# Attention with other halves transposed on TensorE, five low parts on VectorE, x's parts issued later, the first dense tiles placed anew, and w_out's last tile decoded into another buffer

## Chip, cores, metric

The kernel runs on one core of one Trainium2 chip. The metric is the device time of one execution in microseconds; lower is better.

## What is computed

Causal attention over 2 batches, 12 heads, 448 positions and a head size of 64, then a mixer over positions and channels, then a gated layer:

```python
scores = np.where(mask, -1e9, scale * q @ k.T)           # causal, softmax over keys
x = softmax(scores) @ v                                  # to (2, 448, 768)
h = np.maximum(xt @ w_tok1, 0.0) @ w_tok2                # xt: positions last; 448 -> 256 -> 448
u = x + h.transpose(0, 2, 1)
x = u + np.maximum(u @ w_ch1, 0.0) @ w_ch2               # 768 -> 1536 -> 768
h = gelu(x @ w_in)                                       # 768 -> 1024
uu, v = h[..., :512], h[..., 512:]
v_n = (v - mu) / sqrt(var + 1e-6) * g_ln
gated = uu * (w_sg @ v_n + b_sg)                         # over positions
out = x + gated @ w_out                                  # 512 -> 768
```

## The kernel before

**Precision.** Every operand is split into a high and a low part, and each product is three matmuls (hi by hi, hi by lo, lo by hi): `mm3`, L204 to L211. The weights come from memory as eight-byte words into `wraw` and are decoded in three steps (`decode`, L119): ScalarE writes `wm`, VectorE shifts it (L133) and puts in the low bits (L134). Then ScalarE copies the high part and GpSimd subtracts for the low part (`sub`, L103).

**Attention** works on pairs of heads; pair (b,n) is heads 2n and 2n+1 of batch b, `hd` is which of the two, and each head has two halves (`HALVES`, L229), of 512 columns of scores together. For each half `probabilities` (L349) lets TensorE write the scores (`s_ps`, two buffers, L367), VectorE add the mask and take the row maximum (L372: `pe`, `mx`), ScalarE take the exponential (L381). Then the half is transposed on one of two ways. By DMA: ScalarE copies the high part of `hl` (L393), GpSimd writes the low one (L394), SP issues the transpose into `pT` (L395). Or by TensorE (`on_pe`, L383): four transposes into `t_ps` (L387), the high copy on ScalarE (L389), the low part on VectorE (L390). `ON_PE` (L67) says which pairs do this, always for half 1 of head 1. `values` (L408) multiplies `pT` with v into `x_ps` (L418 to L420). At the end of a pair (L446 to L458) VectorE normalises into `xf`, ScalarE copies `xh`, GpSimd makes `xl` and the remaining pieces of `xh`. After two pairs `token_mix` (L460) runs: `a_ps` (L465, then mm3), and then `u_ps` and its parts `uh`, `ul`.

**v.** `prepare_v` (L507) loads v, VectorE takes its absolute maximum (`am`, L336), TensorE spreads it (`vm`, L338), VectorE makes the scale `sv` and the low part `vl` (L344).

**Order.** A scheduler orders every engine's instructions by program order and by the priority that `tc.high_priority(offset=...)` gives; a negative offset lets work give way to what comes after it. `tc.issue_after` puts an instruction behind another. Every DMA, the transposes included, is issued by SP in its own order. The first products with w_ch1 (`r_ps`) fill TensorE during attention: `THIRDS` (L66) says after which head how many thirds of a tile are issued (`up_third`), `BEHIND` (L65) behind which head's transpose each tile's load stands, `LATER` (L64) is the offset of that load's work. `up` takes the rest of the eight tiles NF0 after attention.

**After attention** the r tiles of w_ch1 run, then y with w_ch2, the gelu with w_in, the spatial gate `g_ps` (L855 to L872), and `o_ps` with w_out (L884). w_out's tiles are decoded one at a time by `begin16` into `wm` (three buffers), with a maximum (`wams`, L176), and scaled by `end16` (L198 to L202). At the end of a batch's gate `top_of` (L178) reduces four maxima `gtam` to one, which TensorE spreads into `gt_ps` (L188); `gate16` (L840) then splits the gate into `gt_hi` and `gt_lo` (L196).

Of the kernel before, what the change touches and what calls it, by code (L numbers as in the profile page):

```python
# [15 lines left out]
ALU = mybir.AluOpType  # L16
# [12 lines left out]
def mixer_kernel(  # L29
# [34 lines left out]
    LATER = 0  # L64
    BEHIND = [11, 13, 17, 16, 14, 15, 13, 15]  # L65
    THIRDS = {15: 2, 17: 1, 18: 2, 19: 1, 20: 2, 21: 2, 22: 3, 23: 2}  # L66
    ON_PE = [(0, 1), (0, 2), (0, 3), (0, 4), (0, 5), (1, 0), (1, 1), (1, 2), (1, 4)]  # L67
# [88 lines left out]
    def load_w(src, pool=wpool, bufs=3, behind=None):  # L156
# [7 lines left out]
        else:  # L164
# [3 lines left out]
            w = WC // 3  # L168
            for i in range(3):
                cs = slice(i * w, (i + 1) * w)  # L170
                sub(lo1[:, cs], m[:, cs], hi1[:, cs])
# [102 lines left out]
    with ExitStack() as at:  # L274
# [74 lines left out]
        def probabilities(qp, k2, hd, half, on_pe):  # L349
# [44 lines left out]
            nc.gpsimd.tensor_sub(hl[:, 1], pe, hl[:, 0])  # L394
# [27 lines left out]
        def pair(b, n, e, qk, x, on_pe):  # L422
# [3 lines left out]
            for hd in range(2):  # L426
                if (b, n) != (0, 0):
                    vh, vl, sv = vss[b, n]
                    for half in range(2):
                        values(px, probabilities(*qk, hd, half, on_pe and (hd, half) == (1, 1)), hd, half, vh, vl)  # L430
                else:
                    pTs = []
                    for half in range(2):
                        pTs.append(probabilities(*qk, hd, half, False))
# [19 lines left out]
            for h in range(2):
                hs, ls = (slice(64 * i, 64 * i + 64) for i in (h, 1 - h))
                ds = slice(e * P + h * D, e * P + h * D + D)
                nc.gpsimd.tensor_scalar(xh[hs, 0, ds], xf[hs, e, 0], 1.0, 0.0, ALU.mult, ALU.add)
                sub(xh[ls, 0, ds], xf[hs, e, 0], xh[hs, 0, ds])  # L458
# [62 lines left out]
        def up_third():  # L521
# [8 lines left out]
            with tc.high_priority(offset=-400):  # L530
# [17 lines left out]

        last_mx, last_s, v_begun, tok_raw = [None], [None], {}, {}
# [8 lines left out]
        for n, (b, h) in enumerate(order):  # L558
# [7 lines left out]
            if n == 2:  # L566
                with tc.high_priority(offset=-50):
# [265 lines left out]
    begin16(w_out[NDC + 1], NDC + NDC + 1)  # L833
# [110 lines left out]
```

## Time and profile before

| what | value |
|---|---|
| median of 3 runs | 412.0 us (411.12 to 412.44) |
| profiled execution | 410.7 us |
| its span, first to last instruction | 408.9 us |
| mean granted clock of TensorE | 0.996 |
| TensorE busy | 389.2 us (95%) |
| VectorE busy | 292.2 us (71%) |
| ScalarE busy | 250.7 us (61%) |
| GpSimd busy | 196.9 us (48%) |

The profiled execution is 1.3 us below the median of the runs, and its span leaves out 1.8 us around the instructions. TensorE is the busiest engine by far. A share of 95% is a mean over the program, though: the stretches show where the rest lies, and the list of waits what it waits for. In the rows, PE is TensorE, DVE VectorE, ACT ScalarE, POOL GpSimd, SP the engine that issues the DMAs.

### The profile page before, as it was taken

To read this page: it belongs to the slowest core of one execution; us is meant where nothing else is said; L and a number is where in the kernel's file an instruction comes from. 1 tells how busy PE (TensorE), PEld (TensorE's weight loads), DVE (VectorE), ACT (ScalarE), POOL (GpSimd) and SP (SyncE) were. 2 spreads that over 40 slices of the span, in tenths; PEclk is the share of its full clock that TensorE was granted. 3 is DMA by queue.
4 is the path that set the end of the run, shared out by engine and by line. 5 is a ranking of instruction groups with operands and counts; after the bars stand their busy time and mean duration, and the time that the engine had idled before them with its cause. 6 is when DMAs were issued, how large, how long until landed. Compare 5 with 4: busy or idle time off the path is not lost.

```text
span 408.9 us, 7351 instructions
## 1 busy us (share of the span) xinstructions
PE 389.2 (95%) x2638; PEld 267.5 (65%) x2638; DVE 292.2 (71%) x702; ACT 250.7 (61%) x479; POOL 196.9 (48%) x218
## 2 busy tenths in 40 slices
PE   5898899889998999999999999999999999998996
PEld 3565778678887989999887555555544445554454
DVE  5988986876885625534468787787799997569842
ACT  3887887686977546636689894534177265654200
POOL 3766775696889564341351355254112168315300
PEclk9998999999999999999999999999999999999999
DMA  7999989979967944556733403644621331100123
GB/s 237 207 231 239 229 168 230 231 145 262 226 184 171 232 158 127 183 179 212 243 102 115 145 11 96 206 136 128 230 61 31 103 104 52 53 1 0 69 97 106
DMA packets 57525, 60.74 MB, mean 149 GB/s; under 512 B 43665, under 2 KB 49041, under 8 KB 57489
## 3 DMA queue, kind: packets, MB, share of 16 engines
q1 hardware_dynamic: 57488, 60.28, 55.8%
q8 instruction: 21, 0.34, 0.3%
q14 instruction: 16, 0.12, 0.1%
HBM read 47.29 MB, written 2.75 MB: 122 GB/s over the span
## 4 chain that ended last, share of the span: by engine, by line
DVE 24%; ACT 15%; PE 14%; DMA 11%; issue 5%; POOL 4%; ACTq 0%; SPq 0%; POOLq 0%; DVEq 0%
DMA wraw<-in 11%; ACT r L195 3%; DVE wm L134 3%; PE o_ps L209 2%; ACT w L200 2%; PE o_ps L210 2%; DVE w2m L134 2%; PE o_ps L208 2%; DVE y L196 2%; DVE w2m L133 2%; ACT wm L130 2%; PE r_ps L208 2%; PE r_ps L209 2%; PE r_ps L210 1%; ACT w2m L130 1%
## 5 line engine op out<-in xcount | busy, mean ns | idle before, releaser
L367 PE MATMUL s_ps<-k,q 128*128 128x64 f32 (+3 forms) x216 | 54.9, 399 | 7.2 <-DMA q<-in 4.7
L104 POOL TENSOR_TENSOR wlo<-wm,whi 128x256 fp32r<-128x256 f32 (+1 forms) x36 | 42.4, 1198 | 37.1 <-ACT whi L143 32.1
L394 POOL TENSOR_TENSOR hl<-pe,hl 128x512 f16<-128x512 f32 x39 | 48.4, 1251 | 13.6 <-ACT hl L393 13.0
L208 PE MATMUL r_ps<-uh,whi 128*128 128x448 f32 x144 | 54.1, 377 | 0.0
L209 PE MATMUL r_ps<-ul,whi 128*128 128x448 f32 x144 | 53.3, 370 | 0.0
L210 PE MATMUL r_ps<-uh,wlo 128*128 128x448 f32 x144 | 52.9, 367 | 0.0
L208 PE MATMUL y_ps<-r,w 128*128 128x448 f16 x144 | 50.6, 353 | 0.0
L209 PE MATMUL y_ps<-r,w 128*128 128x448 f16 x144 | 50.6, 352 | 0.0
L210 PE MATMUL y_ps<-r,w 128*128 128x448 f16 x144 | 50.4, 352 | 0.0
L133 DVE TENSOR_SCALAR wm<-wm 128x768 int32<-128x768 int32 (+2 forms) x35 | 21.4, 612 | 38.4 <-ACT wm L130 38.4
L130 ACT ACTIVATE wm<-wraw 128x768 f32<-128x768 f32 (+2 forms) x35 | 27.8, 797 | 34.2 <-DMA wraw<-in 27.8
L367 PEld LDWEIGHTS s_ps<-k,q 128*128 128x128 f32 x216 | 31.4, 203 | 14.3 <-DVE vh L306 4.6
L372 DVE CUSTOM_DVE_ANT_0 pe<-s_ps,mask 128x192 f32<-128x192 f32 (+3 forms) x84 | 34.4, 442 | 5.6 <-PE s_ps L367 5.3
L134 DVE SCALAR_TENSOR_TENSOR wm<-wraw,wm 128x768 int32<-128x768 int32 (+2 forms) x35 | 37.6, 1074 | 0.6
L269 POOL TENSOR_TENSOR y<-yt,ul 128x448 f32<-128x448 f32 x10 | 13.2, 1323 | 42.3 <-DVE yt L267 42.3
L381 ACT ACTIVATE pe<-pe,bias 128x448 f32<-128x448 f32 (+3 forms) x66 | 31.5, 528 | 0.3
L418 PE MATMUL x_ps<-vh,pT 128*128 128x65 f16 (+1 forms) x240 | 25.9, 197 | 4.5 <-DMA pT<-hl 3.4
L209 PEld LDWEIGHTS r_ps<-ul,whi 128*128 128x128 f32 x144 | 27.1, 188 | 3.0 <-issue 0.6
L208 PEld LDWEIGHTS r_ps<-uh,whi 128*128 128x128 f32 x144 | 27.0, 188 | 2.8 <-issue 0.4
L210 PEld LDWEIGHTS r_ps<-uh,wlo 128*128 128x128 f32 x144 | 27.0, 188 | 2.7 <-issue 0.2
L202 POOL TENSOR_TENSOR w<-w2m,w 128x768 f16<-128x768 f32 x12 | 20.6, 1731 | 16.1 <-ACT w2m L201 13.2
L418 PEld LDWEIGHTS <-pT 128*128 128x128 f16 (+1 forms) x240 | 21.5, 99 | 10.3 <-DMA pT<-hl 4.8
(214 smaller groups left out, 1033.5 us busy)
## 6 DMA issues: line engine op xcount, KB each, us to landing
wraw<-in SPq DMA_DIRECT2D x36, 768.0 KB, 4.5
wraw<-in SPq DMA_DIRECT2D x14, 512.0 KB, 3.7
vr<-in SPq DMA_DIRECT2D x12, 320.0 KB, 4.3
k<-in SPq DMA_DIRECT2D x12, 224.0 KB, 3.7
q<-in SPq DMA_DIRECT2D x24, 112.0 KB, 3.9
out<-ob SPq DMA_DIRECT2D x11, 224.0 KB, 2.0
wraw<-in SPq DMA_DIRECT2D x3, 256.0 KB, 3.4
sgr<-in SPq DMA_DIRECT2D x3, 224.0 KB, 2.8
```

Source lines behind the costliest of these rows:

```text
L104: nc.gpsimd.tensor_sub(lo, src, f32(hi))
L130: nc.scalar.activation(m, words.bitcast(F32)[:, :, 1], AF.Prelu, scale=2.0 ** -112, alpha=-(2.0 ** 32))
L133: nc.vector.tensor_scalar(mi, mi, 3, None, ALU.logical_shift_left)
L134: nc.vector.scalar_tensor_tensor(mi, words[:, :, 0], 29, mi, ALU.logical_shift_right, ALU.bitwise_or)
L208: nc.tensor.matmul(ps, lh, rh, start=i == 0 and not begun, stop=False)
L209: nc.tensor.matmul(ps, lh, rl, start=False, stop=False)
L210: done.append(nc.tensor.matmul(ps, ll, rh, start=False, stop=ended and i == n - 1).ins)
L367: last_s[0] = nc.tensor.matmul(ps[:, o:o + m], qp[:, q0:q0 + P], k2[:, ks], start=True, stop=True).ins
L372: last_mx[0] = nc.vector.tensor_tensor_reduce(out=pe[:, cs], in0=ps[:, cs], in1=mask0 if i == 0 else mask[:, MASKS[i]], scale=-1.0 / math. ...
L381: nc.scalar.activation(pe[:, cs], pe[:, cs], AF.Exp, bias=bias[:, j:j + 1], scale=-1.0)
L394: nc.gpsimd.tensor_sub(hl[:, 1], pe, hl[:, 0])
L418: nc.tensor.matmul(o, ph, vh[:, c, h, :D + 1], start=j == 0, stop=False)
```

## The change

Which halves are transposed on TensorE is now a list of halves: (0,1), (1,1), (1,2) and (0,5) keep half 1 of head 1, (0,5) has half 1 of head 0 besides, and in (0,2), (0,3), (0,4), (1,0) it is another half than before; (1,4) has none any more. It is 9 halves as before. Five of the halves that go by DMA have their low part made by VectorE (`LO_DVE`), and two pairs have `xl` made there (`XL_DVE`). The parts of x and the token mix are put on a list `later` and are issued `DEFER` heads later, and in some pairs (`PINX`) behind the last low part that GpSimd made. The low part of a dense tile is one instruction of 768 columns, not three of 256. The numbers that place the r thirds and their loads are others; there are 18 thirds (six tiles) instead of 15 (five). tok2 is loaded after head 3 instead of 2, without an offset, and `prepare_v`'s offset is -40. At the end, w_out's last tile is decoded into `w3`, the buffer of the last tile of w_in (L747), and the first gt of batch 1 is put behind the top of batch 0.

```diff
-    LATER = 0
-    BEHIND = [11, 13, 17, 16, 14, 15, 13, 15]
-    THIRDS = {15: 2, 17: 1, 18: 2, 19: 1, 20: 2, 21: 2, 22: 3, 23: 2}
-    ON_PE = [(0, 1), (0, 2), (0, 3), (0, 4), (0, 5), (1, 0), (1, 1), (1, 2), (1, 4)]
+    LATER = 800
+    BEHIND = [11, 13, 17, 17, 12, 12, 18, 15]
+    DEFER = [2, 0, 0, 1, 0, 0, 2, 1, 0, 1, 1, 0]
+    PINX = [1, 0, 0, 0, 0, 1, 1, 0, 1, 0, 1, 1]
+    THIRDS = {15: 2, 17: 1, 18: 3, 19: 3, 20: 3, 21: 2, 22: 1, 23: 3}
+    ON_PE = [(0, 1, 1, 1), (0, 2, 0, 1), (0, 3, 0, 0), (0, 4, 0, 1), (0, 5, 0, 1), (0, 5, 1, 1), (1, 0, 1, 0), (1, 1, 1, 1), (1, 2, 1, 1)]
+    LO_DVE = [(0, 4, 1, 0), (0, 4, 1, 1), (1, 0, 0, 0), (1, 3, 1, 1), (1, 5, 1, 1)]
+    XL_DVE = [(0, 2), (1, 4)]
...
-            w = WC // 3
-            for i in range(3):
+            w = WC // 1
+            for i in range(1):
...
-            nc.gpsimd.tensor_sub(hl[:, 1], pe, hl[:, 0])
+            ins = (nc.vector if lo_dve else nc.gpsimd).tensor_sub(hl[:, 1], pe, hl[:, 0]).ins
+            if not lo_dve:
+                last_hl[0] = ins
...
-                        values(px, probabilities(*qk, hd, half, on_pe and (hd, half) == (1, 1)), hd, half, vh, vl)
+                        values(px, probabilities(*qk, hd, half, (b, n, hd, half) in ON_PE, (b, n, hd, half) in LO_DVE), hd, half, vh, vl)
...
+            x6 = xf[:, e, 1:].rearrange("p (c h) d -> p c (h d)", h=2)
+            later.append((count_n[0] + DEFER[6 * b + n], lambda: x_parts(b, n, e, x6, xf, xh, xl)))
+
+        def x_parts(b, n, e, x6, xf, xh, xl):
             cs = slice(e * P, (e + 1) * P)
-            x6 = xf[:, e, 1:].rearrange("p (c h) d -> p c (h d)", h=2)
             nc.scalar.copy(xh[:, 1:, cs], x6)
-            sub(xl[:, :, cs], x6, xh[:, 1:, cs])
...
+            with tc.issue_after(last_hl[0]) if PINX[6 * b + n] else nullcontext():
+                (nc.vector if (b, n) in XL_DVE else nc.gpsimd).tensor_sub(xl[:, :, cs], x6, f32(xh[:, 1:, cs]))
...
-                with tc.high_priority(offset=-80):
+                with tc.high_priority(offset=-40):
                     vr, _ = v_begun.pop(n, None) or load_v(b, h // 2)
...
-            with tc.high_priority(offset=-400):
+            with tc.high_priority(offset=-800):
                 mm3(
...
-            if n == 2:
-                with tc.high_priority(offset=-50):
+            if n == 3:
+                with nullcontext():
                     for c in range(NT):
                         load_tok2(c)
...
-                token_mix(b, h // GH, *x)
+                later.append((n + DEFER[n // 2], lambda b=b, g=h // GH, x=x: token_mix(b, g, *x)))
+            while later and (later[0][0] <= n or n == len(order) - 1):
+                later.pop(0)[1]()
...
-    begin16(w_out[NDC + 1], NDC + NDC + 1)
+    begin16(w_out[NDC + 1], NDC + NDC + 1, w3[:, :NDC * P])
...
-            nc.vector.scalar_tensor_tensor(gt, pg[:, :S], gcol[:, m:m + 1], bb, ALU.mult, ALU.add)
+            with tc.issue_after(last_top[0]) if (b, m) == (1, 0) else nullcontext():
+                nc.vector.scalar_tensor_tensor(gt, pg[:, :S], gcol[:, m:m + 1], bb, ALU.mult, ALU.add)
```

How the instructions stand at three places. First TensorE, between the values of pair (0,1) (`vh_177`) and the first values of pair (0,2) (`vh_172`); `k_604` are the scores of pair (0,4). Before:

```order
L419 MATMUL x_ps<-vl_181,pT 128x64
L420 LDWEIGHTS pT
L420 MATMUL x_ps<-vh_177,pT 128x65
L387 MATMUL t_ps<-ident,pe 128x128 x4
L367 MATMUL s_ps<-k_604,q_164 128x128
L367 MATMUL s_ps<-k_604,q_164 128x64
L367 MATMUL s_ps<-k_604,q_164 128x320
L367 MATMUL s_ps<-k_604,q_164 128x448
L418 LDWEIGHTS pT
```

After:

```order
L425 MATMUL x_ps<-vl_181,pT 128x64
L426 LDWEIGHTS pT
L426 MATMUL x_ps<-vh_177,pT 128x65
L391 MATMUL t_ps<-ident,pe 128x128 x4
L371 MATMUL s_ps<-k_604,q_164 128x64
L371 MATMUL s_ps<-k_604,q_164 128x448
L371 MATMUL s_ps<-k_604,q_164 128x128
L371 MATMUL s_ps<-k_604,q_164 128x64
L371 MATMUL s_ps<-k_604,q_164 128x320
L424 LDWEIGHTS pT
```

Before, t_ps is the second half of pair (0,2)'s second head, and its first head's second half goes by DMA; after, t_ps is that second half of the first head, and the first scores of (0,4) (64 and 448 columns) have moved behind it.

SP near the same place, from the transposes of pair (0,2) to those of pair (0,3). Before:

```order
L395 DMA_TRANSPOSE pT<-hl 128x8x128 x2
L329 DMA vr<-in 128x640
L321 DMA k_958<-in 128x448
L323 DMA q_163<-in 64x448 x2
L323 DMA q_164<-in 64x448
L116 DMA wraw<-in 128x512
L395 DMA_TRANSPOSE pT<-hl 128x8x128
L329 DMA vr<-in 128x640
L395 DMA_TRANSPOSE pT<-hl 128x8x128
L321 DMA k_1110<-in 128x448
L323 DMA q_164<-in 64x448
L395 DMA_TRANSPOSE pT<-hl 128x8x128
```

After:

```order
L401 DMA_TRANSPOSE pT<-hl 128x8x128
L333 DMA vr<-in 128x640
L401 DMA_TRANSPOSE pT<-hl 128x8x128
L327 DMA q_163<-in 64x448 x2
L333 DMA vr<-in 128x640
L327 DMA q_164<-in 64x448
L325 DMA k_1110<-in 128x448
L120 DMA wraw<-in 128x512
L327 DMA q_164<-in 64x448
L401 DMA_TRANSPOSE pT<-hl 128x8x128 x3
L327 DMA q_165<-in 64x448
L325 DMA k_1313<-in 128x448
```

The last three transposes of each list are those of pair (0,3): before, loads stand between them; after, the three stand in a row, with the loads of wraw, q and k ahead of them.

VectorE at the row maxima of pair (1,2)'s second head, first half (`pe_155`, `mx_157`); `am` is the reduction of a v tile, `wm` a decode. Before:

```order
L494 TENSOR_TENSOR ul_0_112<-u_ps,uh_0_100 128x448
L336 TENSOR_REDUCE am<-vr 128x1
L133 TENSOR_SCALAR wm<-wm 128x768
L446 TENSOR_SCALAR rd<-x_ps,sv 128x7
L134 SCALAR_TENSOR_TENSOR wm<-wraw,wm 128x768
L447 RECIPROCAL rd<-rd 128x7
L372 ISA pe_155,mx_157<-s_ps,mask 128x448
L372 ISA mx_157 128x1
L344 SCALAR_TENSOR_TENSOR vl_176<-vr,sv,vh_172 128x640
L448 TENSOR_TENSOR xf<-x_ps,rd 128x448
L372 ISA pe,mx<-s_ps,mask 128x192
```

After:

```order
L452 TENSOR_SCALAR rd<-x_ps,sv 128x7
L453 RECIPROCAL rd<-rd 128x7
L454 TENSOR_TENSOR xf<-x_ps,rd 128x448
L376 ISA pe_155,mx_157<-s_ps,mask 128x448
L376 ISA mx_157 128x1
L348 SCALAR_TENSOR_TENSOR vl_176<-vr,sv,vh_172 128x640
L394 SCALAR_TENSOR_TENSOR pT<-t_ps,pT 128x512
L137 TENSOR_SCALAR wm<-wm 128x768
L138 SCALAR_TENSOR_TENSOR wm<-wraw,wm 128x768
L340 TENSOR_REDUCE am<-vr 128x1
L376 ISA pe,mx<-s_ps,mask 128x192
```

The maximum has moved ahead of am and of both steps of the decode.

VectorE where w_out's last two tiles are decoded, up to the first gt; `w_4033` is the last tile's new place. Before:

```order
L189 TENSOR_REDUCE winv<-w_ps 128x1
L134 SCALAR_TENSOR_TENSOR wm<-wraw,wm 128x512
L190 TENSOR_SCALAR winv<-winv 128x1
L176 TENSOR_REDUCE wams<-wm 128x1
L191 RECIPROCAL wsc<-winv 128x1
L133 TENSOR_SCALAR wm<-wm 128x512
L134 SCALAR_TENSOR_TENSOR wm<-wraw,wm 128x512
L176 TENSOR_REDUCE wams<-wm 128x1
L189 TENSOR_REDUCE winv<-w_ps 128x1
L190 TENSOR_SCALAR winv<-winv 128x1
L191 RECIPROCAL wsc<-winv 128x1
L869 SCALAR_TENSOR_TENSOR gt<-g_ps,gcol,bb 128x448
```

After:

```order
L838 SCALAR_TENSOR_TENSOR sgl<-sgr,sgs,sgh 128x448 x4
L137 TENSOR_SCALAR w_4033<-w_4033 128x512
L138 SCALAR_TENSOR_TENSOR w_4033<-wraw,w_4033 128x512
L180 TENSOR_REDUCE wams<-w_4033 128x1
L137 TENSOR_SCALAR wm<-wm 128x512
L193 TENSOR_REDUCE winv<-w_ps 128x1
L138 SCALAR_TENSOR_TENSOR wm<-wraw,wm 128x512
L194 TENSOR_SCALAR winv<-winv 128x1
L180 TENSOR_REDUCE wams<-wm 128x1
L195 RECIPROCAL wsc<-winv 128x1
L193 TENSOR_REDUCE winv<-w_ps 128x1
L194 TENSOR_SCALAR winv<-winv 128x1
```

Before, the last decode (its three steps) stands right before winv and the first gt; after, the last tile's three steps stand ahead of the decode of the tile before it.

## Rows read from the trace of the kernel before

**Rows 1.** Stretches: window, its length, busy per engine (instructions), PEclk, DMA share, GB/s
```profile
30.00:60.00 30.00, 26.72 (x294) 20.90 (x293) 26.26 (x78) 24.97 (x62) 22.46 (x29) 0.94 0.99 215
60.00:90.00 30.00, 27.29 (x284) 22.46 (x284) 22.95 (x72) 23.14 (x50) 21.13 (x28) 1.00 1.05 208
...
160.00:372.00 212.00, 211.60 (x1094) 131.64 (x1094) 152.85 (x318) 128.21 (x212) 77.95 (x58) 1.00 0.37 121
```
**Rows 2.** TensorE's waits: waiting line, releaser, us in total, times, longest
```profile
PE x_ps L418 <- DMA pT<-hl: 3.4, 3, 1.6
PE s_ps L367 <- DVE mx L372: 2.6, 3, 1.3
PE gt_ps L188 <- DVE gtam L181: 1.6, 1, 1.6
...
PE a_ps L465 <- POOL xh L104: 0.9, 1, 0.9
```
**Rows 3.** TensorE in time: start, us, instruction, count [idle before it <-releaser]
```profile
36.66 0.20 PE L418 MATMUL x_ps<-vh,pT 128*128 128x65 f16 x1 [1.61 <-DMA pT<-hl]
...
50.45 0.20 PE L418 MATMUL x_ps<-vh,pT 128*128 128x65 f16 x1 [1.56 <-DMA pT<-hl]
...
85.63 1.24 PE L367 MATMUL s_ps<-k,q 128*128 128x64 f32 x4 [1.27 <-DVE mx L372]
...
128.04 0.39 PE L465 MATMUL a_ps<-xh,w1h 128*128 128x256 f32 x1 [0.87 <-POOL xh L104]
```
**Rows 4.** Two stretches around 37 us, columns as in group 1
```profile
30.00:37.00 7.00, 5.28 (x62) 3.50 (x61) 6.71 (x23) 7.00 (x19) 4.02 (x7) 1.00 1.10 219
37.00:41.00 4.00, 4.00 (x26) 2.71 (x23) 2.41 (x7) 1.53 (x6) 3.73 (x5) 0.61 0.86 256
```
**Rows 5.** VectorE in time ahead of 85 us, columns as in group 3
```profile
82.82 0.69 DVE L336 TENSOR_REDUCE am<-vr 128x1 bf16<-128x512 f32 x1 [1.85 <-DMA vr<-in]
...
84.02 0.95 DVE L134 SCALAR_TENSOR_TENSOR wm<-wraw,wm 128x768 int32<-128x768 int32 x1
```
**Rows 6.** Groups by form, 0 to 160 us: busy us, mean ns, idle before
```profile
L394 POOL TENSOR_TENSOR hl<-pe,hl 128x512 f16<-128x512 f32 x39 | 48.4, 1251 | 13.6 <-ACT hl L393 13.0
L104 POOL TENSOR_TENSOR wlo<-wm,whi 128x256 fp32r<-128x256 f32 x24 | 19.0, 819 | 2.2 <-ACT whi L167 2.2
...
L494 DVE TENSOR_TENSOR ul<-u_ps,uh 128x448 fp32r<-128x448 f32 x10 | 6.0, 611 | 3.7 <-ACT uh L493 3.7
```
**Rows 7.** VectorE, and GpSimd beside it, from 43 to 50 us
```profile
43.37 0.68 DVE L134 SCALAR_TENSOR_TENSOR wm<-wraw,wm 128x512 int32<-128x512 int32 x1
...
47.45 1.63 DVE L134 SCALAR_TENSOR_TENSOR wm<-wraw,wm 128x512 int32<-128x512 int32 x1
...
46.09 4.01 POOL L394 TENSOR_TENSOR hl<-pe,hl 128x512 f16<-128x512 f32 x3
```
**Rows 8.** Chain that ended last, 104 to 129 us: start, us, what
```profile
115.02 4.39 DMA wraw<-in
...
122.62 1.17 DVE vl L344
```
**Rows 9.** Chain that ended last, 355 to 382 us
```profile
363.33 0.44 DVE wm L133
363.79 0.70 DVE wm L134
364.51 0.69 DVE wams L176
...
377.65 0.59 DVE gt L869
```
**Rows 10.** TensorE in time at 378 us
```profile
378.88 0.35 PE L209 MATMUL o_ps<-gt_lo,wh 128*128 128x448 f16 x1 [0.40 <-DVE gt_lo L196]
```
**Rows 11.** GpSimd and TensorE in time from 170 to 173 us
```profile
170.00 1.87 POOL L104 TENSOR_TENSOR wlo<-wm,whi 128x768 fp32r<-128x768 f32 x1 [8.66 <-ACT whi L143]
...
172.90 0.37 PE L208 MATMUL r_ps<-uh,whi 128*128 128x448 f32 x1
```

More of the change, by code (lines that the diff above doesn't have):

```diff
@@ L347, in mixer_kernel, with probabilities @@
         count = [0]
-        def probabilities(qp, k2, hd, half, on_pe):
+        def probabilities(qp, k2, hd, half, on_pe, lo_dve):
             ps = ps_s.tile([P, NP], F32, tag="s", name="s_ps")
@@ L420, in values, with pair @@
                         last_x[0] = nc.tensor.matmul(o, pl, vh[:, c, h, :D + 1], start=False, stop=j == i).ins
-        def pair(b, n, e, qk, x, on_pe):
+        def pair(b, n, e, qk, x):
             xf, xh, xl = x
@@ L433, in pair @@
                     for half in range(2):
-                        pTs.append(probabilities(*qk, hd, half, False))
+                        pTs.append(probabilities(*qk, hd, half, False, False))
                         if hd == 0:
@@ L448, in pair @@
             nc.vector.tensor_mul(xf[:, e], px[:, :, :D], rd.to_broadcast([P, 7, D]))
+            x6 = xf[:, e, 1:].rearrange("p (c h) d -> p c (h d)", h=2)
+            later.append((count_n[0] + DEFER[6 * b + n], lambda: x_parts(b, n, e, x6, xf, xh, xl)))
+        def x_parts(b, n, e, x6, xf, xh, xl):
             cs = slice(e * P, (e + 1) * P)
-            x6 = xf[:, e, 1:].rearrange("p (c h) d -> p c (h d)", h=2)
             nc.scalar.copy(xh[:, 1:, cs], x6)
-            sub(xl[:, :, cs], x6, xh[:, 1:, cs])
[L454 to L458, printed above, removed]
+            with tc.issue_after(last_hl[0]) if PINX[6 * b + n] else nullcontext():
+                (nc.vector if (b, n) in XL_DVE else nc.gpsimd).tensor_sub(xl[:, :, cs], x6, f32(xh[:, 1:, cs]))
+                for h in range(2):
+                    hs, ls = (slice(64 * i, 64 * i + 64) for i in (h, 1 - h))
+                    ds = slice(e * P + h * D, e * P + h * D + D)
+                    nc.gpsimd.tensor_scalar(xh[hs, 0, ds], xf[hs, e, 0], 1.0, 0.0, ALU.mult, ALU.add)
+                    sub(xh[ls, 0, ds], xf[hs, e, 0], xh[hs, 0, ds])
         def token_mix(b, g, xf, xh, xl):
@@ L547, in decode_tok @@
                 load_tok(c, tok_raw[c])
+        later, count_n = [], [0]
+        last_hl = [None]
         last_mx, last_s, v_begun, tok_raw = [None], [None], {}, {}
@@ L576, in mixer_kernel @@
             if h % 2 == 0:
-                it = pair(b, h // 2, h % GH // 2, qks[b, h // 2], x, (b, h // 2) in ON_PE)
+                it = pair(b, h // 2, h % GH // 2, qks[b, h // 2], x)
+            count_n[0] = n
             next(it, None)
```

## Prediction

> **What bounds the kernel now.** I read the profile from coarse to fine. The stretches of the span come first [rows 1]: from 160 to 372 us TensorE works 211.60 of 212.00 us, so nothing that the change does there can be seen except by starting it earlier. In attention it is idle for 3.28 us between 30 and 60 and for 2.71 between 60 and 90. That is what attention can give, besides the clock. Then TensorE's waits [rows 2]: 3.4 us for transposes that come by DMA, 2.6 for a row maximum from VectorE, 1.6 for the absolute maximum at the end, 0.9 for a part of x from GpSimd. The single instructions say where [rows 3]: at 36.66 (second half of head 0 of pair (0,2)), at 50.45 (pair (0,3), first half of its second head) and at 85.63 (scores behind a row maximum). The granted clock [rows 4] shows a second loss that stands in no list of waits: from 37 to 41 its mean is 0.61, with TensorE busy all 4.00 us. Full clock is 2.4 GHz and the lower level 1.2 GHz; a mean of 0.61 is some 3.1 us at the lower one. Ahead of it TensorE had worked only 5.28 of 7.00 us, and its last 1.61 of idleness is the wait at 36.66.
>
> Up to the fifth group's token mix (a_ps at 128.04, [rows 3]) both kernels let TensorE do the same work in all, though in another order, and from there on TensorE does not stop before 372. So I forecast how far 128.04 moves, whether that shift passes through to the end, and what the end itself gives.
>
> **Attention: other halves by TensorE.** Both kernels transpose 9 of 48 halves on TensorE and 39 by DMA, so neither engine gets more work: four halves stay, five change places.
>
> The second half of pair (0,2)'s head 0 is now among them. Its DMA transpose is what 36.66 waits for, 1.61 us [rows 3]. The new t_ps stands in TensorE's order ahead of the next scores, so the result should be there in time. But two scores buffers now have to come free in another order, and a wait for a maximum can stand where the wait for the transpose was. Bounds 0 to -1.6; I take -1.0, nearer the full wait.
>
> The clock: at full speed the 4.00 busy microseconds would have been 0.61 x 4.00 = 2.44, so 1.56 is lost [rows 4]. If the idle stretch ahead of it goes, the fall may go with it; if a shorter idle stretch is enough, it stays. Bounds 0 to -1.6 (it could also fall elsewhere, which is why I don't count on it all); I take -1.0.
>
> At 50.45 the wait is again for a DMA transpose, 1.56 us [rows 3]. Pair (0,3) now has its first half on TensorE and its last three through SP one behind the other, where before one stood between other loads. The transposes are three in either kernel, so the wait may stay. Bounds 0 to -1.56; I take -0.4.
>
> **VectorE's order at 85 us.** The wait of 1.27 at 85.63 [rows 3] is for a row maximum, and ahead of it in VectorE's queue stood a reduction of v that itself waited 1.85 us for its load, and a decode whose second step took 0.95 and ended at 84.97 [rows 5]. Now the maximum stands ahead of both (the order of VectorE's instructions below the diff shows it). TensorE is then bound by its own previous work. Bounds -0.9 to -1.27; I take -1.2.
>
> **Work moved from GpSimd to VectorE.** Five low parts leave GpSimd: 5 x 1.251 = 6.3 us [rows 6]. The low parts of w_ch1 there are no longer made in three pieces: 24 x 0.819 = 19.7 become 8 x 1.87 = 15.0 [rows 6, 11], 4.7 less. But GpSimd ends TensorE's idleness for 0.9 us only [rows 2], and its relief is worth no more than that, which I count below. VectorE gets five operations of 128x512 with both sources in SBUF, and two of 128x384 for x. Its nearest rows are 0.611 for 128x448 (one source in PSUM), so about 0.68 each by size and 0.52 for the two: 5 x 0.68 + 2 x 0.52 = 4.4 us. The upper bound is shown by the same decode step twice [rows 7]: 0.68 at 43.37, when GpSimd was idle, and 1.63 at 47.45, when GpSimd was in a run of three low parts (46.09 for 4.01). At that price it is 5 x 1.63 + 2 x 1.22 = 10.6. In attention VectorE waits more often than TensorE waits for it (2.6 us in all); most of the seven lie beside TensorE's work. I take +0.8, about one of them on the path; bounds 0 and 8.2 (all five low parts, contended).
>
> By the Trainium skill, page "SBUF — State Buffer", section "Who interferes with whom", a VectorE instruction with two SBUF inputs and a GpSimd instruction that reads SBUF shut each other out for the whole instruction. The pair of 0.68 and 1.63 agrees. By that rule a low part on VectorE does not relieve GpSimd's line at no cost: it takes its turn with the GpSimd work that it was to run beside. Its consequence is the slower rival below.
>
> **x's parts behind later low parts, r and its loads.** The parts of x and the token mix are now issued up to two heads later, and in some pairs behind the last GpSimd low part of the head. That lets GpSimd serve transposes first and keeps the in-order queue of SP from standing behind a part of x. TensorE's idle time ahead of the fifth token mix is 0.87 us, for such a part [rows 3]. Its last links were the third load of w_ch1 (115.02 for 4.39), a decode and the low part of v (122.62 for 1.17), and only then the maximum [rows 8]. After the change that low part no longer stands ahead of the maximum, but the load and the decode do, and SP issues that load at nearly the same place. So of 0.87 and a wait for a maximum just before it I take -0.2, bounds 0 and -1.6. What is late next is the load itself. The dense tiles in thirds are six of eight, five before: TensorE has the same products before 128.04, so this costs 0.
>
> Attention in sum: -1.0 -1.0 -0.4 -1.2 +0.8 -0.2 = -3.0.
>
> **Does the shift pass through?** The tight spot is the twelfth tile of w_ch1: its low part ended at 170.00 + 1.87 = 171.87, and its first product began at 172.90 [rows 11], 1.0 us of slack. The loads wait for buffers that TensorE's products free, so the chain moves with TensorE. I take 0, bounds 0 and +2.0 (3.0 less the slack).
>
> **The end.** At the end VectorE runs without a gap from a decode of w_out's last tile (363.33) to the gt that its last low part waits for (377.65) [rows 9]. The decode now goes into a free part of another buffer and stands before, not inside this stretch; it was 0.44 + 0.70 + 0.69 = 1.83 us [rows 9]. Besides, the first gate's top goes ahead of a gt of 0.59 [rows 9], so the wait of 1.6 for it [rows 2] goes too. What is late next is gt_lo: TensorE waits 0.40 for it today [rows 10], and a TensorE that gets there sooner waits longer, since gt_lo stands behind VectorE's gt and maximum as before. So the gains don't add up to 1.83 + 0.59: 1.6 + 0.4 = 2.0 is all that TensorE waits there, and I leave 0.6 of it, one VectorE step of 0.59, for gt_lo: -1.4, bounds -0.8 (two such steps left) and -2.0.
>
> **Sum.** -3.0 + 0 - 1.4 = -4.4. The profiled execution took 410.7 us, so 406.3 on its scale; the median of the runs is 412.0, 1.3 above it, so **407.6 us**.
>
> **Rivals.**
> Slower: VectorE becomes the bound of attention between 60 and 90 us, where several of the five low parts now lie and where TensorE's longest wait is on VectorE already [rows 3, 5]. At the contended 1.63 each [rows 7], all five on the path: 8.2 in place of 0.8. Gains ahead of it -3.8, the end -1.4, so +3.0: 415.0. It decides from 5.2 us on the path, three of the five contended; at that point the gains are used up. For it: 1.63 against 0.68. Against it: VectorE works 22.95 of 30.00 us there [rows 1] and has room for 4.4.
>
> Attention stays where it is: the load of 115.02 and not the waits before it sets 128.04 [rows 8], and each removed wait turns into a longer one at the fifth token mix. Only the end is left: 412.0 - 1.4 = 410.6. For it: the chain goes through two loads, one behind the other. Against it: these loads are issued behind transposes, which come earlier when the heads do.
>
> All waits go: 1.61 + 1.56 + 1.56 + 1.27 + 0.87 = 6.9 in attention, 2.0 at the end: 403.1. Against it: a removed wait seldom leaves nothing behind in a pipeline with two scores buffers.
>
> That the change does not do what it says is excluded by the order of the instructions: the transposes, the maximum and the decode do stand elsewhere.
>
> **How the numbers follow.** The forecast 0.56, slower 0.13, attention unmoved 0.14, all waits 0.12; 0.05 is left for mixtures that I can't name. About 0.3% (1.2 us) is what a measurement of this kernel can tell from no change. Faster by more: most of the forecast (0.53), half of the unmoved case (0.07, it lies at 0.34%), all waits (0.12), 0.01 of the rest: 0.73. Slower by more: 0.13 and 0.01. The same: 0.13. The range is 403.0 to 412.5: it leaves out the slower case (0.13) and, beyond all waits, some 0.06. Its upper end is the forecast with +2.0 for the pass-through and three more uncontended low parts on the path (2.0), and a little for the spread of the runs.
>
> **What would show it.** Right: no wait for a transpose near 36, a granted clock of 1.0 from 37 to 41, no wait for a maximum near 84, the fifth token mix near 125.0, no wait between it and some 369, and a gap of about 0.6 before the first low gate product. Wrong: an idle TensorE with VectorE's low parts (0.68 by my estimate) at 1.2 or more between 60 and 90 us; the token mix still at 128; the half clock at another place; a wait in r for a low part of w_ch1 near 169.

## Result and profile after

The changed kernel takes 405.06 us (median of 4 runs, 404.51 to 407.86) where the kernel before takes 412.22: ratio 0.9854, 95% interval 0.9808 to 0.9900. Beside later experiments on another occasion (run f3 below) it took 407.02, ratio 0.9898 (0.9862 to 0.9935). All nine runs together have a median of 406.7, the 61 runs of the kernel before that stand beside the experiments 412.1. Five of these 61 are in a slower state that some executions fall into, and the ratios leave such runs out. The forecast was 407.6, range 403.0 to 412.5.

The profiled execution took 404.83 us with a span of 403.0; before it was 408.9. The largest of TensorE's waits (line waited at, releaser, sum, times, longest) answer to [rows 2]:

```profile
PE s_ps L371 <- DMA q<-in: 4.6, 1, 4.6
PE x_ps L424 <- DMA pT<-hl: 2.8, 3, 1.4
PE u_ps L491 <- ACT ah L480: 1.5, 1, 1.5
PE x_ps L424 <- DVE xf L454: 0.6, 2, 0.4
PE s_ps L371 <- DVE mx L376: 0.5, 2, 0.3
PE a_ps L213 <- POOL xl L462: 0.4, 1, 0.4
```

The wait for the gate's maximum (1.6) is gone, the one for transposes fell from 3.4 to 2.8, the one for row maxima from 2.6 to 0.5. A new one is the 1.5 for `ah`, the high part of the token mix; behind it stands a row maximum again, as the section on the prediction shows. The stretches (columns as in [rows 1, 4]) show the same:

```profile
30.00:60.00 30.00, 27.03 (x320) 20.97 (x319) 27.00 (x77) 24.11 (x58) 20.64 (x27) 1.00 1.02 224
60.00:90.00 30.00, 27.85 (x312) 23.32 (x311) 24.04 (x72) 23.00 (x49) 19.35 (x22) 1.00 1.03 194
...
157.00:372.00 215.00, 215.00 (x1115) 134.03 (x1114) 158.58 (x331) 131.44 (x218) 83.40 (x64) 1.00 0.36 116
...
37.00:41.00 4.00, 2.77 (x49) 1.96 (x48) 2.21 (x9) 1.91 (x6) 1.43 (x3) 1.00 1.27 184
```

In attention TensorE is busy 0.3 and 0.6 us more of each 30, and gets through more in it (320 instructions in place of 294 from 30 to 60); from 157 to 372 it never waits; and from 37 to 41 its granted clock is 1.00, that is 2.4 GHz throughout, where it was 0.61.

Since TensorE's work after attention is the same, instruction for instruction, its starts can be set side by side. (Up to the fifth token mix the two traces have 1113 and 1119 matmuls, so that row compares nearly the same work too.) This table is worked out from both traces:

| TensorE's first | before | after | shift | gained since the row above |
|---|---|---|---|---|
| a_ps of the fifth group | 128.04 | 125.23 | -2.8 | 2.8 |
| y_ps | 221.26 | 218.51 | -2.75 | 0 |
| v_ps | 303.38 | 300.63 | -2.75 | 0 |
| ug_ps | 331.60 | 328.10 | -3.5 | 0.75 |
| g_ps | 359.12 | 355.62 | -3.5 | 0 |
| o_ps | 377.75 | 372.44 | -5.3 | 1.8 |
| end | 408.91 | 403.05 | -5.9 | 0.55 |

So the gain of this pair of profiles has three places: attention 2.8, the product with w_in's v half 0.75, the gate and what follows it 2.35.

### The profile page after: what moved, and what is told of

Same layout as the page of the kernel before. It is cut to its first block, busy times and chain, and to the rows that moved or that the text cites. A ratio compares the mean times of both kernels' runs of the same rounds, so it can differ in the third digit from the quotient of the medians.

```text
span 403.0 us, 7341 instructions
## 1 busy us (share of the span) xinstructions
PE 387.5 (96%) x2638; PEld 267.2 (66%) x2638; DVE 296.7 (74%) x709; ACT 249.9 (62%) x479; POOL 188.8 (47%) x195
## 3 DMA queue, kind: packets, MB, share of 16 engines
HBM read 47.29 MB, written 2.75 MB: 124 GB/s over the span
## 4 chain that ended last, share of the span: by engine, by line
PE 73%; DVE 12%; DMA 7%; ACT 3%; issue 2%; SPq 1%; POOL 1%; DVEq 0%; ACTq 0%; POOLq 0%
PE y_ps L214 7%; PE y_ps L212 7%; PE y_ps L213 7%; PE r_ps L212 6%; PE r_ps L214 6%; PE r_ps L213 6%; DMA vr<-in 3%; DVE pe L376 3%; PE o_ps L212 2%; PE o_ps L214 2%; PE ug_ps L213 2%; PE ug_ps L214 2%; PE o_ps L213 2%; PE ug_ps L212 2%; PE v_ps L213 2%; PE v_ps L212 2%
## 5 line engine op out<-in xcount | busy, mean ns | idle before, releaser
L108 POOL TENSOR_TENSOR wlo<-wm,whi 128x768 fp32r<-128x768 f32 x20 | 42.9, 2147 | 35.5 <-ACT whi L147 31.8
L398 POOL TENSOR_TENSOR hl<-pe,hl 128x512 f16<-128x512 f32 x34 | 42.2, 1245 | 18.3 <-ACT hl L397 14.9
L137 DVE TENSOR_SCALAR wm<-wm 128x768 int32<-128x768 int32 (+2 forms) x34 | 22.7, 668 | 29.6 <-ACT wm L134 29.6
L138 DVE SCALAR_TENSOR_TENSOR wm<-wraw,wm 128x768 int32<-128x768 int32 (+2 forms) x34 | 33.1, 973 | 0.7
```

The source lines that it names most:

```text
L108: nc.gpsimd.tensor_sub(lo, src, f32(hi))
L137: nc.vector.tensor_scalar(mi, mi, 3, None, ALU.logical_shift_left)
L138: nc.vector.scalar_tensor_tensor(mi, words[:, :, 0], 29, mi, ALU.logical_shift_right, ALU.bitwise_or)
L398: ins = (nc.vector if lo_dve else nc.gpsimd).tensor_sub(hl[:, 1], pe, hl[:, 0]).ins
```

## Experiments

### The end: which of the two edits

Three kernels have only the edits at the end, and one all but them.

```diff
e1, e2:
-    begin16(w_out[NDC + 1], NDC + NDC + 1)
+    begin16(w_out[NDC + 1], NDC + NDC + 1, w3[:, :NDC * P])
e1, e3:
-            nc.vector.scalar_tensor_tensor(gt, pg[:, :S], gcol[:, m:m + 1], bb, ALU.mult, ALU.add)
+            with tc.issue_after(last_top[0]) if (b, m) == (1, 0) else nullcontext():
+                nc.vector.scalar_tensor_tensor(gt, pg[:, :S], gcol[:, m:m + 1], bb, ALU.mult, ALU.add)
e4: the changed kernel with both of these taken back
```

Both edits:

> The kernel before with the two edits at the end alone: w_out's last tile decoded into w3, and the first gt of batch 1 behind the top of batch 0. Theory (the end is a matter of its own: VectorE's decode of 0.44 + 0.70 + 0.69 us stood in its line and TensorE waited 1.56 for the gate's maximum and 0.40 for gt_lo): both waits gone, everything up to the first g_ps where it was (359.1 us), o_ps some 1.8 us earlier and the end 2.3 us earlier: ratio to before 0.9945, about 410.0 where before is 412.2. Rival (the end gains only because attention is over earlier and the loads of w_out have more lead): a wait of over 0.8 us stays in the gate, the gain is under 1.2 us (0.997 or more).

The last tile's place alone:

> The kernel before with w_out's last tile decoded into w3, nothing else. Theory: the decode is the whole of it, since VectorE's line from 363.3 to 378.2 has no gap and loses 1.8 us: the end 1.8 to 2.3 us earlier (0.9945 to 0.9955), the wait of gt_ps for the maximum 0.3 or less. Rival (the top behind gt is half of it): gt_ps still waits 0.6, the end 1.2 to 1.6 us earlier (0.996 to 0.997).

The order of the top alone:

> The kernel before with the first gt of batch 1 behind the top of batch 0, nothing else. Theory: gt_ps waits 0.5 us less (1.0 in place of 1.56), but the scale of the gate stands on VectorE behind a maximum that waits for GpSimd's product with that same gt, so gt_lo comes no sooner and o_ps waits as much more: no change in the time (0.999 to 1.001). Rival: the gate's maximum is what counts, so 0.6 us are gained (0.9985).

All but these two:

> The changed kernel without the two edits at the end. Theory (parts independent): attention gives 2.8 us at the fifth token mix as in the changed kernel, 0.7 more where y is split for v, and in the gate the waits of before come back (1.5 for the maximum, 0.4 for gt_lo): 3.5 us under before (0.9915), 408.7. Rival (loads that come sooner also bring the decode of w_out's last tile sooner, so that the waits at the end would have gone anyway): under 0.8 us of waits in the gate, the time within 0.5 us of the changed kernel's (0.986 to 0.987).

| run | ratio to before (95%) | from the first g_ps to the end, us |
|---|---|---|
| before | 1 | 49.79 |
| e1, both | 0.9954 (0.9931 to 0.9976) | 47.44 |
| e2, w3 alone | 0.9948 (0.9916 to 0.9980) | 47.43 |
| e3, top alone | 1.0015 (0.9978 to 1.0052) | 49.85 |
| e4, neither, rest changed | 0.9888 (0.9845 to 0.9931) | 49.20 |
| changed | 0.9854 (0.9808 to 0.9900) | 47.43 |

The right column is sharper than the times, for nothing ahead of the gate enters it. It is needed: e1's first g_ps stands at 362.26 and not at 359.1 as expected, though nothing ahead of it was edited, and e3's interval holds both its theory and its rival. Alone, the decode's new place gives all of the 2.36 us, and the order of the top nothing, as the theory for e3 said. In e3 TensorE's wait is 0.5 shorter at gt_ps and longer at o_ps:

```profile
374.76 0.23 PE L188 MATMUL gt_ps<-ident_b,gtam 128*128 128x128 bf16 x1 [1.08 <-DVE gtam L181]
378.64 0.73 PE L208 MATMUL o_ps<-gt_hi,wh 128*128 128x448 f16 x3 [0.43 <-ACT gt_hi L195]
379.77 0.35 PE L209 MATMUL o_ps<-gt_lo,wh 128*128 128x448 f16 x1 [0.41 <-DVE gt_lo L196]
```

Why the whole wait goes with w3 alone, gt_lo's too, is seen on VectorE in e2 (start, us, instruction, idle before it):

```profile
371.69 0.68 DVE L869 SCALAR_TENSOR_TENSOR gt<-g_ps,gcol,bb 128x448 f32<-128x448 f32 x1
372.29 0.15 DVE L181 TENSOR_REDUCE gtam<-gtam 128x1 bf16<-128x4 f32 x1
373.77 0.69 DVE L869 SCALAR_TENSOR_TENSOR gt<-g_ps,gcol,bb 128x448 f32<-128x448 f32 x1 [1.33 <-PE g_ps L210]
```

Without the decode VectorE has done its line by 372.4 and then waits 1.33 us for TensorE. The two have changed places: gt_lo is no longer queued behind a late line. e4 lies between theory (49.8) and rival: 49.20. The decodes of w_out stand 0.6 us earlier there, seen from the first g_ps, and the wait at gt_ps is 0.97 in place of 1.56. So in the changed kernel the two edits are worth 1.8 us and the rest of the change 0.6; which part of the rest moves the decodes was not tested.

### Attention: halves, low parts, x's parts, loads

```diff
e5: the changed kernel with
+    ON_PE = [(b, n, 1, 1) for b, n in [(0, 1), (0, 2), (0, 3), (0, 4), (0, 5), (1, 0), (1, 1), (1, 2), (1, 4)]]
e6: the changed kernel with
+    LO_DVE = []
+    XL_DVE = []
e7: the changed kernel with
+    DEFER = [0] * 12
+    PINX = [0] * 12
e8: the changed kernel with the old LATER, BEHIND, THIRDS and
-            with tc.high_priority(offset=-800):
+            with tc.high_priority(offset=-400):
...
-            w = WC // 1
-            for i in range(1):
+            w = WC // 3
+            for i in range(3):
e10: the kernel before with the new ON_PE
```

The old halves:

> The changed kernel with the halves of before on TensorE (half 1 of head 1 in nine pairs); all else as changed. Theory (the prediction's terms for the halves: -1.0 for the transpose at 36.7, -1.0 for the clock, -0.4 for the transpose at 50): 2.4 us slower than the changed kernel, ratio to before 0.991; the wait of some 1.6 us for a DMA transpose in pair (0,2) is back, and the half clock behind it in the profile or in most of the runs. Rival (the halves only move the waits about, and loads and x's parts give the gain): within 0.6 us of the changed kernel, 0.984 to 0.987.

The low parts on GpSimd:

> The changed kernel with all low parts of the halves and all of xl on GpSimd. Theory (the prediction: 0.8 us of VectorE's seven operations lie on the path, and GpSimd's relief gives nothing): 0.8 us faster than the changed kernel, ratio to before 0.9835. First rival (no effect, all seven lie beside TensorE's work): 0.9845 to 0.987. Second rival (GpSimd's line is what the transposes wait for in SP's order, 6.3 us shorter in the changed kernel): the transposes of the five halves come later, 1.5 us or more slower, 0.989 or more, with a wait of x_ps for a transpose at 60 to 80 us.

x's parts at once:

> The changed kernel with x's parts and the token mix issued at once and behind no low part (DEFER and PINX all 0). Theory (the prediction's -0.2): at most 0.5 us slower than the changed kernel, 0.9855 to 0.987. Rival (GpSimd serves x's parts ahead of the low parts again, and SP stands behind them as it did before, 7 us and more of its waits): 1.5 us or more slower, 0.989 or more, with longer waits for transposes.

The old loads:

> The changed kernel with the loads and thirds of r as before: LATER 0, the old BEHIND and THIRDS, offset -400, the low part in three pieces of 256. Theory (the loads' lead after attention comes from their new place; in the changed kernel the decode of the tiles after attention stands 4 to 6 us earlier, more than TensorE's 2.75): attention the same within 0.5 us, but the lead is gone, and the waits in y and v of before (0.75 in the profile) come back: ratio to before 0.987 to 0.988. First rival (nothing, the lead comes from attention being over sooner): 0.985 to 0.986. Second rival (GpSimd's 4.7 us for the pieces and the fifth token mix's wait for x's parts): attention 1.5 us slower, 0.989.

The new halves alone:

> The kernel before with the new choice of halves for TensorE, nothing else. Theory (the prediction's terms for the halves stand by themselves: -1.0, -1.0, -0.4): fifth token mix 2.4 us sooner, ratio to before 0.994, no wait for a transpose near 36.7. Rival (the choice of halves fits one order of the instructions only, as the 13 us suggest that came when the old halves were put into the changed kernel): no gain or a loss, 1.000 or more, with waits for transposes at other halves.

| run | median, us | ratio to before (95%) |
|---|---|---|
| e5, old halves | 418.39 | 1.0129 (1.0064 to 1.0194) |
| e6, low parts on GpSimd | 419.50 | 1.0151 (1.0074 to 1.0229) |
| e7, x's parts at once | 407.40 | 0.9877 (0.9806 to 0.9947) |
| e8, old loads | 410.84 | 0.9947 (0.9906 to 0.9988) |
| e10, new halves alone | 413.08 | 1.0041 (1.0004 to 1.0078) |

e5 and e6 missed every expectation by far. Taking back either of these two parts makes the kernel slower than before, by 5 to 8 us, and slower than the changed one by some 11 to 14. The halves alone (e10) gain nothing and lose a little, as the rival said, with 8.3 us of waits for transposes in seven places where the kernel before has 3.4 in three. e7 lies between its theory and its rival; it is 0.4 us slower than f3 below, and its waits for transposes (2.1 us in all) are not longer than the changed kernel's, so the rival's mark is missing. e8 missed too, and is taken up in the next section. In e5 TensorE waits for transposes nine times, 13.8 us in all. Two rows of TensorE in e5 and two in e6 show the kind of waits:

```profile
83.65 0.27 PE L424 MATMUL x_ps<-vh,pT 128*64 128x65 f16 x2 [4.21 <-DMA pT<-hl]
...
135.84 0.24 PE L424 MATMUL x_ps<-vh,pT 128*128 128x65 f16 x1 [3.20 <-DMA pT<-hl]
```

```profile
116.64 0.23 PE L424 MATMUL x_ps<-vh,pT 128*128 128x65 f16 x1 [3.04 <-DMA pT<-hl]
...
163.66 0.58 PE L474 MATMUL a_ps<-xh,w1h 128*128 128x256 f32 x1 [4.55 <-POOL xh L108]
```

Waits of 3 to 4.6 us, and the lower clock behind them (0.83 as a mean from 110 to 130 and from 150 to 170 in e6):

```profile
110.00:130.00 20.00, 16.94 (x125) 13.72 (x124) 14.19 (x37) 17.25 (x38) 16.65 (x15) 0.83 1.00 236
130.00:150.00 20.00, 20.00 (x162) 18.00 (x161) 8.96 (x22) 13.23 (x29) 13.45 (x15) 1.00 0.80 173
150.00:170.00 20.00, 14.69 (x117) 12.65 (x117) 5.54 (x8) 6.41 (x13) 9.32 (x9) 0.83 0.44 130
```

In e6 the two waits and the clock behind them come to 3.04 + 4.55, and 0.17 of 20 us twice, 14.4 in all: about what its span is longer than the changed kernel's (14.1). The chain before 116.64 reads like the second rival: two low parts on GpSimd, a low part of w_ch1 behind them, SP, and then the transpose itself (start, us, what):

```profile
102.33 2.90 POOL hl L398 x2
105.30 2.19 POOL wlo L108
107.49 1.92 SPq L401
...
110.13 6.46 DMA pT<-hl
```

But the rival's own mark, a wait between 60 and 80 us, is missing (0.28 at 61.92 is all that stands there), and neither long wait is at one of the five halves (the first is at the half before the fourth of them). Nor is GpSimd short of time: it stood idle shortly before both waits, 3.41 us up to 102.33 and 4.29 up to 157.05. Before the second one, the pieces of xh that TensorE waits for stand in its queue behind a low part of w_ch1:

```profile
157.05 1.83 POOL L108 TENSOR_TENSOR wlo<-wm,whi 128x768 fp32r<-128x768 f32 x1 [4.29 <-ACT whi L147]
...
160.22 1.80 POOL L108 TENSOR_TENSOR wlo<-wm,whi 128x768 fp32r<-128x768 f32 x1 [0.20 <-POOL xh L466]
162.10 1.51 POOL L108 TENSOR_TENSOR xh<-xf,xh 64x64 fp32r<-64x64 f32 x2
```

In the changed kernel the same pieces stand ahead of that low part. This points to the order of the instructions, and the comparison is not clean for that reason. The order is made by a scheduler from program order and priorities. If the traces are set beside the changed kernel's, 484 of TensorE's 2638 matmuls lie outside the longest order that the two have in common in e5, and 466 in e6. (Single entries move the order as much: counted on the programs as built, of 4232 weight loads and matmuls, one half moved back in pair (0,2) displaces 355, the low part of (1,0) alone 501; neither was run.) So e5 and e6 can't show what a transpose or a low part is worth by itself. In e7 it is 39, so x's parts were tested with the order nearly kept.

Two more entries could be moved so: two low parts (f1, 22 matmuls) and one half (f2, 19). They ran beside the changed kernel (f3).

```diff
f1:
-    LO_DVE = [(0, 4, 1, 0), (0, 4, 1, 1), (1, 0, 0, 0), (1, 3, 1, 1), (1, 5, 1, 1)]
+    LO_DVE = [(0, 4, 1, 0), (1, 0, 0, 0), (1, 3, 1, 1)]
f2: in ON_PE
-    (0, 4, 0, 1)
+    (0, 4, 1, 1)
```

> The changed kernel with two of the five low parts back on GpSimd, (0,4,1,1) and (1,5,1,1); TensorE's order stays but for 52 of 4234 rows, SP's wholly. Theory (what cost 13 us with all seven on GpSimd was the order that came with it, and two low parts beside TensorE's work cost nothing on either engine): within 0.8 us of the changed kernel on the same chip, waits for transposes as there. Rival (GpSimd's line is what SP's transposes wait for): each of the two transposes lands 0.6 us or more later, and TensorE waits for them; 1.2 us or more slower than the changed kernel, ratio to it 1.003 or more.

> The changed kernel with pair (0,4)'s second half of head 1 on TensorE in place of the second half of head 0 (the low part of the one now on DMA is GpSimd's); TensorE's order stays but for 44 rows of 4234. Theory (which half goes by TensorE decides where TensorE waits: a half whose DMA transpose would land last): a wait of 0.8 us or more for a transpose at the second half of head 0 near 57 us, and the time 0.5 to 1.5 us above the changed kernel's. Rival (with the order kept, the choice of half is worth nothing): within 0.4 us of it.

> The changed kernel once more, beside the three others on one chip: ratio to before 0.983 to 0.988, and in about half of the runs a granted clock of 1.000 over the whole span, where the kernel before has it seldom.

| run | median, us | ratio to before (95%) |
|---|---|---|
| f1, two low parts on GpSimd | 407.89 | 0.9928 (0.9888 to 0.9968) |
| f2, one half moved | 406.83 | 0.9878 (0.9833 to 0.9922) |
| f3, changed | 407.02 | 0.9898 (0.9862 to 0.9935) |

With the order kept, neither can be told from the changed kernel: f2 is 0.2 us below it, f1 0.9 above, and the intervals overlap. f1's 0.9 is just outside its theory's 0.8 and short of the rival's 1.2. The rival's mark is missing in it: TensorE waits for transposes once, for 1.6 at 41.14, ahead of both low parts. The longest wait of its profile, 2.5 for `ah` at 91.93, comes from elsewhere: VectorE had waited for the load of a v tile, with the next row maxima behind it.

```profile
89.43 0.69 DVE L340 TENSOR_REDUCE am<-vr 128x1 bf16<-128x512 f32 x1 [3.32 <-DMA vr<-in]
```

In f2 no wait for a transpose stands near 57. f3 missed its own expectation: its ratio is above the range, and one of its five runs has a clock of 1.000, not half of them.

So for this half and these two low parts the choice is worth nothing that the runs can tell. The other halves and low parts were not tested with the order kept. That the 11 to 14 us of e5 and e6 come from the order is argued from these runs and from e6's rows, not shown by an experiment that changes the order alone.

### The loads' lead after attention

e8 also answers for the 0.75 us in v. The time from the first v_ps to the first ug_ps falls into two classes, by the loads:

| profiles | first y_ps to first v_ps, us | first v_ps to first ug_ps, us |
|---|---|---|
| old loads: before, e1, e2, e3, e8, e10 | 82.12, 83.47, 82.53, 83.66, 82.39, 83.04 | 28.22, 28.33, 28.33, 28.32, 28.32, 28.32 |
| new loads: changed, e4, e5, e6, e7, f1, f2, f3 | 82.12 in all eight | 27.73 in f1, 27.47 or 27.48 in the other seven |

So v's 0.75 to 0.85 us belongs to the placing of the first r tiles and their loads and not to attention's earlier end (e5 ends attention 11 us later than before and has it too). And there is more of it than the profile of before showed: with the old loads y loses up to 1.5 us, in five of six profiles, with the new ones nothing. The longest waits of e1 in y and v say on what:

```profile
PE rs_ps L188 <- DVE ram L181: 0.5, 1, 0.5
PE v_ps L210 <- DVE y L196: 0.4, 1, 0.4
PE y_ps L208 <- ACT w L200: 0.3, 1, 0.3
```

How it comes is seen on ScalarE, whose high parts for v stand behind a decode that waits for its load. Before:

```profile
295.26 0.93 ACT L130 ACTIVATE wm<-wraw 128x768 f32<-128x768 f32 x1 [6.11 <-DMA wraw<-in]
```

After:

```profile
289.81 0.91 ACT L134 ACTIVATE wm<-wraw 128x768 f32<-128x768 f32 x1 [5.91 <-DMA wraw<-in]
```

It starts 5.45 us earlier while TensorE is 2.75 earlier: 8.1 us ahead of the first v_ps before, 10.8 after. From that decode on, ScalarE and VectorE do the same in the same order up to the first low part of y for v: it starts 0.14 us behind the first v_ps before, and 2.35 ahead of it after. The mean of the old row of y is 82.87, so with v the new loads are worth about 1.5 us after attention, by an estimate from these six profiles (0.75 + 0.8). Which of LATER, BEHIND, THIRDS, the offset and the one-piece low part gives the lead was not taken apart.

e8's other expectations, attention the same within 0.5 us and a ratio of 0.987 to 0.988, failed. In its profile TensorE waits 2.58 us for a transpose at 23.79 and 2.27 at 128.58. The first can't come from the edit: up to 74 us every engine has the same instructions in the same order as in the changed kernel. By the fourth token mix nothing of it is left (100.47 against 100.19 in the changed kernel and 101.78 in f3). From there to the first y_ps e8 takes 123.84, the other two 118.33 and 118.11. That loss of 5.5 us is about the second wait and the lower clock behind it, 2.27 and 0.34 of 10 us:

```profile
127.00:137.00 10.00, 8.42 (x58) 7.64 (x59) 6.14 (x12) 6.20 (x14) 5.97 (x7) 0.66 0.88 248
```

So most of what e8 loses lies in the last part of attention and not in y and v. 81 of TensorE's 2638 matmuls are displaced there; whether the old loads or that order makes the wait stays open.

## Why the prediction was right, step by step

**Attention: -3.0 forecast, -2.8 in the profile, but the size is partly luck.** The fifth token mix starts at 125.23. In f3, the same program, it starts at 126.66, and in four profiles that have the old attention (before, e1, e2, e3) at 128.04, 129.70, 129.36 and 127.25. Differences of 1 to 2 us are what one execution may show; the means (128.6 against 125.9 with e4's 125.67) give -2.7. That sum is measured. How it divides among the terms is not shown, since no experiment took them apart. What the rows say of each:

- The transposes (-1.0 and -0.4). At 36.7 the wait is gone as forecast, and it has moved to the half that TensorE gave up in exchange, (0,2)'s second half of head 1:

```profile
40.31 0.20 PE L424 MATMUL x_ps<-vh,pT 128*128 128x65 f16 x1 [1.23 <-DMA pT<-hl]
```

All waits for transposes fell by 0.6 (1.0 in f3), not 1.4. That a half that is put on TensorE sends another to the DMA, and that this one may then be the late one, was missing in the step. The wait at 50.45 is gone in the profile after, but in f3 the same half makes TensorE wait 1.54 at 50.19. In the old attention it is the larger of the two and not the smaller: 3.04, 2.62 and 1.90 in e1, e2 and e3, against 1.32, 0.89 and 1.08 for the one near 36.

- The clock (-1.0). 1.00 from 37 to 41 in the profile after, as said; but in f3 it fell at another place, behind that wait at 50.19, which the prediction had named as a sign of being wrong:

```profile
52.00:56.00 4.00, 4.00 (x16) 3.07 (x16) 2.45 (x9) 3.25 (x7) 1.16 (x1) 0.61 1.10 220
```

The old attention's profiles do the same: it falls behind the wait near 50 in e1 and e2 (a mean of 0.72 from 50 to 56 and from 48 to 54) and not at all in e3 (1.00 from 30 to 60). Three of the nine runs of the changed kernel have a mean clock of 1.000, of the 61 runs of before 10. Those 10 have a median of 411.0, the 30 runs with 0.996 one of 412.0. So an execution with a fall takes about 1.0 us longer, with whatever wait stands ahead of the fall. That the change makes a fall rarer is not shown by nine runs; 1.0 for each execution was too much.

- The maximum at 85 (-1.2). No wait there any more. Instead TensorE waits 1.50 at 89.81 for the high part of the token mix, which ScalarE makes, where the prediction had it "bound by its own previous work". The cause is the old one, one step further on: VectorE's next reduction of v waits for its load, the next row maxima stand behind it, ScalarE waits for them, and `ah` stands behind ScalarE's exponentials:

```profile
87.31 0.69 DVE L340 TENSOR_REDUCE am<-vr 128x1 bf16<-128x512 f32 x1 [1.88 <-DMA vr<-in]
87.91 0.35 DVE L376 CUSTOM_DVE_ANT_0 pe<-s_ps,mask 128x192 f32<-128x192 f32 x1
...
88.30 0.97 ACT L385 ACTIVATE pe<-pe,mx 128x192 f32<-128x192 f32 x2 [1.49 <-DVE mx L376]
89.18 0.58 ACT L480 ACTIVATE ah<-a_ps 128x512 fp32r<-128x512 f32 x1
...
89.81 0.47 PE L491 MATMUL u_ps<-w2h,ah 128*128 128x448 f32 x1 [1.50 <-ACT ah L480]
```

The wait follows the load: where the reduction waited 0.54 us for it (f3), TensorE waits 0.2, and where it waited 3.32 (f1), 2.47. So the step took one maximum out from behind a reduction and left the next one there.

- VectorE's seven operations (+0.8). The five low parts took 6.0 us, 0.68 to 1.79 each:

```profile
L398 DVE TENSOR_TENSOR hl<-pe,hl x5: 676/1178/1789, 50.4 to 133.2; 128x512 f16<-128x512 f32 x5
```

With 1.1 for the two xl this is 7.1, between the bounds of 4.4 and 10.6. The one of 1.79 began at 50.40, with GpSimd in a subtraction of 1.29 from 50.35 that reads the same memory:

```profile
50.35 1.29 POOL L108 TENSOR_TENSOR w2l<-wm,w2h 128x512 fp32r<-128x512 f32 x1
```

That fits an instruction that stood still until about 51.64: it ended 0.55 us later, and the shortest of the five took 0.68 in all. The slower rival's price (1.63) does occur, its place doesn't: none of the three waits for transposes in the changed profile (at 22.98, 40.31 and 48.92) is at one of the five halves. Nor do several of the five lie between 60 and 90 us, as the rival has it: one does, at 61.84, and it took 0.68. By the Trainium skill, page "SBUF — State Buffer", section "Who interferes with whom", the pair of ports that VectorE and GpSimd share is an exclusive lock, and a VectorE instruction with two inputs in SBUF contends for it with a GpSimd instruction that reads SBUF. These two rows agree.

- x's parts and the fifth token mix (-0.2): 0.77 and 0.87 became 0.44 (for xl). e7 says that issuing x's parts at once costs nothing that its four runs can tell, which is what the small term said.

**The shift passes through (0, bounds 0 and +2.0).** Through r and y it does, to 0.02 us: -2.75 from 153 us to v (in f3 -1.37, as steadily). The bounds were on the wrong side, though. I asked whether the loads would hold TensorE up and not whether the new placing gives them more lead; it does, and it is worth 0.75 in the profile and about 1.5 in a usual run. With the 0.96 by which the end gave more, it is what the sum lacks: the profiles differ by 5.9 and the medians by 5.4 to 7.2, where 4.4 was forecast.

**The end (-1.4, bounds -0.8 and -2.0): -2.36.** The place and the cause were right; the term is mis-sized, and the gap of about 0.6 that was to remain is not there. The step that failed is "gt_lo stands behind VectorE's gt and maximum as before". I took VectorE's line as the bound after the edit too. With 1.83 us taken out it is no longer late, so its 1.33 us of idleness falls where gt_lo's delay was. The second edit, which I counted as a gain beside the first, gives nothing (e3). The ceiling was too low as well. I took the waits as listed, 1.56 + 0.40, for all there was to gain. But a stop costs more than its listed idle time. Before and after set side by side, the starts move by 1.73 us at the stop of 1.56 and by 0.57 at the stop of 0.40: 2.30 of the 2.36. That fits rows in which matmuls without a stop between them overlap, starting every 0.19 us and lasting 0.35 (e2):

```profile
376.84 0.35 PE L209 MATMUL g_ps<-sgl,z_hi 128*128 128x448 f16 x1
377.03 0.35 PE L210 MATMUL g_ps<-sgh,z_lo 128*128 128x448 f16 x1
```

In the changed kernel about 0.6 of it would have come without the two edits (e4).

**Rivals.** Slower through VectorE: no. Attention unmoved: no; the load at 115 came earlier with the heads, and its decode starts at 117.4 where it was 119.5. All waits gone (403.1): the median of 405.06 lies nearer to this than to the forecast, but the mechanism isn't there. TensorE still waits 2.8 us for transposes and 1.5 for `ah`, and part of the gain comes from behind attention, where this rival has only the end. What none of them had is how near the tables stand to a much worse order.

## To carry over

Where a scheduler orders the work, an entry of a table is not a local edit: price the whole order that results, and don't expect a part of a tuned set to keep its share of the gain, or to be harmless, alone. Where an instruction that waits for a load stands in an engine's queue, look at everything behind it, not only at the one that you move ahead of it. At a stage where two engines run neck and neck, ask after each removal which of them is now the one that waits; what stands behind the other's line then costs nothing. And a placing of loads is worth looking at far behind its own stage, where the lead that it gives or takes shows as small waits.

## What the runs showed of the hardware

The same attention differs by up to 2.4 us from one profile to the next (127.25 to 129.70 at the fifth token mix). The waits for transposes make much of it: in the four profiles of the old attention the long ones stand at the same two halves, but the second is anything from 1.56 to 3.04 us; in the two of the changed kernel the longest stands at 22.98 in one and at 50.19 in the other. The granted clock falls to 1.2 GHz for some 3 us behind one of them, or not at all: in two profiles of the changed kernel it stayed at 1.00 in one and fell between 52 and 56 us in the other. Where TensorE is fed without a gap, the same stretch repeats to 0.01 us (82.12 from the first y_ps to the first v_ps in all eight profiles with the new loads).
